# A feed-forward block in three-part products: another exact split, whose three products add up in one bank

## The chip, the cores and the metric

One core of one Trainium2 chip runs the whole kernel. The metric is the device time of one execution in microseconds (us). TensorE (PE) multiplies matrices, VectorE (DVE), ScalarE (ACT) and GpSimd (POOL) work element by element, and SyncE (SP) issues DMAs. PE writes its sums into PSUM, eight banks of 512 numbers per partition; DVE and ACT read them there.

## The reference

Random features of queries and keys make a linear attention, whose output x (4352 tokens by 128) goes through a gated feed-forward block with 1536 hidden channels:

```python
phi(x) = (S1 x) outer (S2 x)                    # 8 x 8 = 64 features per token and head
x = (phi(q) @ (phi(k).T @ v)) / (phi(q) @ sum(phi(k)) + 1e-6)
g = x @ w_gate
out = (g * (1.0 / (1.0 + np.exp(-g))) * (x @ w_val)) @ w_out
```

Everything is float32; the weights come as float64 and are narrowed on the chip.

## The kernel before

Tokens go in ten blocks: three of 384, 320 and 384 (blocks 0 to 2, batch 0), six of 480 (3 to 8) and one of 384 (9, `LAST`). The hidden channels go in twelve chunks of 128. A *unit* (i, j) is block i and chunk j: gate and value products into two neighbouring banks (a *pair*), Silu of the gate on ACT into `sg`, and the product of `sg` with the value on DVE into a slot of `hidden`. `down` takes the oldest unit from `todo` and adds its share of the output product into a bank of the block. Three pairs (banks 0 and 1, 4 and 5, 6 and 7) go round, the least recently used first (`pair`, L122); a unit holds its pair until `let_go` (L133). Banks 2 ("g2") and 3 ("acc") take the output sums. Attention for batches 1 to 3 runs between the units, step by step (`attentions`, L620): key features on DVE, their sums on POOL (L552), `fold` (L606 to L613), which makes the weights of the query sketches (L347), the sketches' copies on ACT (L595), `query_step` (L757 to L774) and `numerators` (L782), which takes two pairs, 64 small products (L792) and copies into `xT` (L809).

A float32 product of 480 columns is two passes of 0.405 us on PE (L1095). Blocks 0 and 1 and chunks 0 to 5 of block 2 are made so (`unit`, L1035). From unit (2, 6) on, gate and value products are made of *parts* that fit a shorter number format (F32R), in one pass of 0.217 us each. With B = 4096, each weight is w = w1 + wb/B and each token x = x1 + x0; wd = w1 - wb and xd = x1/B - x0. Then w x is (1 + 1/B) times the sum of w1 x1, wb x0 and -wd xd / (1 + 1/B). Of the output products, the 61 units listed in `DOWN` are made in the same way, with parts h1, h0, hd of the hidden unit.

- `start_unit` (L1001) makes both wd xd (L1007), and ACT scales the pair in place (L1010). `finish_unit` (L1012) adds w1 x1 (L1019) and wb x0 (L1020) for gate and value, then Silu (L1022) and product (L1027). In the main loop, unit y + 1 is started before unit y is finished, but at y = 20 and 40 (`WIDE`).
- `cut_weights` (L855) makes the parts of three chunks, one step at a time: w1 (ACT, L859), the rest (L862, DVE or POOL), wb (ACT, L864), wd (L867 on DVE, or L871 on POOL for v0, v2, v3 and g0). The steps are set out by hand in `steps_at` (L1347 to L1399).
- `cut_tokens` (L873) makes the parts of a block's tokens in two steps: x1 on ACT (L881) with x0 (L884, POOL or DVE) and xd (L889, DVE); `token_steps` (L1424) sets the steps of the later blocks, `cuts["x"]` and `x_steps` those of blocks 2 and 3.
- `cut_down` (L925) makes the parts of the output weights; its later steps are in `behind`.
- `cut_hidden` (L960) makes the parts of a unit's output a unit or two later: h1 (ACT L976, or DVE L980), h0 (DVE L984), and hd either on DVE (L990) or, where `carried`, by two DMAs: SP copies h1 to hd (L978) and POOL's accumulating DMA adds h0 (L988).
- `down` (L1072) puts wd hd (L1087) into the block's bank and w1 h1, wb h0 (L1089, L1090) into a second bank of the block, which lies in the other block's bank. ACT copies the second one out with a scale (`copy_out`, L1113), DVE joins both (`put_together`, L1123), and `store` transposes (DVE, L1147) and sends.

The main loop (L1429) runs 84 units, y = 0 to 83, for blocks 3 to 9. `before` and `behind` hold what is to be recorded ahead of or after a unit y. A unit's output product comes when more than 6 units wait (7 at the y in `LONGER`), so some 6 units later. All engines take their instructions in the order in which the code records them. PE's order is that of the code: `group()` at the y in `GROUPS`, the unit's products, then up to two output products.

```python
if y in WIDE:
    finish_unit(*at[0], y)
if y + 1 < END:
    start_unit(*at[1])
if y not in WIDE:
    finish_unit(*at[0], y)
```

Of the kernel before, what the change touches and what calls it, by code (L numbers as in the profile page):

```python
# [19 lines left out]
def kernel(  # L20
# [807 lines left out]
    CUT = 1.0 - 2.0**-13  # L828
    WHOLE = 1.0 + 1.0 / BETA
# [25 lines left out]
    def cut_weights(w, c, low, engine):  # L855

        w1, wb, wd = w_parts[id(w), c] = home(w, c)
        src = w[:, 3 * c : 3 * c + 3, :]
        nc.scalar.activation(out=w1, in_=src, func=AF.Copy, scale=CUT)  # L859
        yield  # L860
        low = low[0]
        engine.tensor_tensor(out=low, in0=src, in1=whole(w1), op=ALU.subtract)  # L862
        yield
        nc.scalar.activation(out=wb, in_=low, func=AF.Copy, scale=BETA)  # L864
        yield
        if engine is nc.vector:
            nc.vector.scalar_tensor_tensor(  # L867
                out=wd, in0=low, scalar=-BETA, in1=whole(w1), op0=ALU.mult, op1=ALU.add
            )
        else:  # L870
            engine.tensor_tensor(out=wd, in0=whole(w1), in1=whole(wb), op=ALU.subtract)  # L871

    def cut_tokens(i, engine=nc.gpsimd, soon=False):  # L873

        t0, n = blocks[i]
        x = xT[:, t0 : t0 + n]
        x1, x0, xd = x_parts[i] = [
            apool.tile([P, WB], F32R, tag=tag, name=name, bufs=2)
            for tag, name in (("qb", "x1"), ("dT", "x0"), ("rd", "xd"))
        ]  # L880
        nc.scalar.activation(x1[:, 0:n], x, AF.Copy, scale=CUT)  # L881

        def low():
            engine.tensor_tensor(  # L884
                out=x0[:, 0:n], in0=x, in1=whole(x1[:, 0:n]), op=ALU.subtract
            )

        def difference():
            nc.vector.scalar_tensor_tensor(  # L889
                out=xd[:, 0:n], in0=whole(x1[:, 0:n]), scalar=WHOLE, in1=x,  # L890
                op0=ALU.mult, op1=ALU.subtract,
            )


        first, second = (difference, low) if soon else (low, difference)
        first()
        yield
        second()
# [26 lines left out]
    def cut_down():  # L925
# [6 lines left out]
        def high(c):  # L932
            nc.scalar.activation(w1[:, c], wo[:, FINE[0] :][:, c], AF.Copy, scale=CUT)

        def left(c):
            nc.gpsimd.tensor_tensor(
                out=wb[:, c], in0=whole(w1[:, c]), in1=wo[:, FINE[0] :][:, c], op=ALU.subtract
            )

        def differ(c):  # L940
            nc.vector.scalar_tensor_tensor(
                out=wd[:, c], in0=whole(wb[:, c]), scalar=BETA, in1=whole(w1[:, c]),
                op0=ALU.mult, op1=ALU.add,
            )

# [6 lines left out]
        add_to(behind, 2, lambda: left(a))  # L952
        add_to(behind, 2, lambda: left(b))
        add_to(behind, 5, lambda: differ(a))
        add_to(behind, 6, lambda: differ(b))
        add_to(behind, 2, lambda: left(c))
        add_to(behind, 21, lambda: differ(c))
        yield

    def cut_hidden(y, i, j):  # L960
# [11 lines left out]
        small = -CUT / BETA  # L972
        carried = i in line[:3] and (i, j) not in [(line[2], 2), (line[2], 8)] or i in line[3:-1] and j % 2
        aside = carried or j % 2 or i in line[:3]
        if aside:
            add_to(behind, y + 1, lambda: nc.scalar.activation(h1, h, AF.Copy, scale=small))  # L976
        if carried:
            add_to(behind, y + 1, lambda: nc.sync.dma_start(out=whole(hd), in_=whole(h1)))  # L978
        if not aside:
            high = lambda: nc.vector.tensor_scalar(h1, h, small, None, op0=ALU.mult)  # L980
            before.setdefault(y + 1, []).insert(0, high)

        def rest():
            nc.vector.scalar_tensor_tensor(  # L984
                out=h0, in0=whole(h1), scalar=BETA, in1=h, op0=ALU.mult, op1=ALU.add
            )
            if carried:
                nc.gpsimd.dma_start(out=hd, in_=h0, accum_op=ALU.add)  # L988
            else:
                nc.vector.tensor_tensor(out=hd, in0=whole(h1), in1=whole(h0), op=ALU.add)  # L990
# [8 lines left out]
    sums_of = {}  # L999

    def start_unit(i, j):  # L1001

        n = blocks[i][1]
        xd = x_parts[i][2][:, 0:n]
        ps = sums_of[i, j] = pair((i, j))[:, :, 0:n]
        for k, w in enumerate((wg, wv)):
            nc.tensor.matmul(  # L1007
                ps[:, k], w_parts[id(w), j // 3][2][:, j % 3, :], xd, start=True, stop=True
            )
        nc.scalar.activation(ps, ps, AF.Copy, scale=-1.0 / WHOLE)  # L1010

    def finish_unit(i, j, y=None):  # L1012
        n = blocks[i][1]
        x1, x0, _ = (x[:, 0:n] for x in x_parts[i])
        ps = sums_of.pop((i, j))
        now(before, y)
        for k, w in enumerate((wg, wv)):
            w1, wb = (w_parts[id(w), j // 3][t][:, j % 3, :] for t in range(2))
            nc.tensor.matmul(ps[:, k], w1, x1, start=False, stop=False, skip_group_check=True)  # L1019
            nc.tensor.matmul(ps[:, k], wb, x0, start=False, stop=True, skip_group_check=True)  # L1020
        sg = fpool.tile([P, WB], FP32, tag="sg", name="sg", bufs=5)[:, 0:n]
        nc.scalar.activation(sg, ps[:, 0], AF.Silu, scale=WHOLE)  # L1022
# [4 lines left out]
        nc.vector.scalar_tensor_tensor(  # L1027
            out=hj[:, 0:n], in0=ps[:, 1], scalar=WHOLE, in1=sg, op0=ALU.mult, op1=ALU.mult
        )
        let_go((i, j))  # L1030
        now(behind, y)
        if (i, j) in DOWN:
            cut_hidden(y, i, j)
# [38 lines left out]
    def down(y=None):  # L1072
# [7 lines left out]
        mine = [c for c in range(NCH) if (i, c) in DOWN]  # L1080
        if mine and j == mine[0]:
            acc[i, "p"] = bank("acc" if i in line[0::2] else "g2")
        sides = dict(start=first, stop=(made[i] == NCH))
        if j in mine:
            w1, wb, wd = [down_parts[x][:, FINE.index(j), :] for x in ("w1", "wb", "wd")]
            h1, h0, hd = h_parts.pop((i, j))
            nc.tensor.matmul(acc[i][:, 0:n], wd, hd, **sides)  # L1087
            p = acc[i, "p"][:, 0:n]
            nc.tensor.matmul(p, w1, h1, start=(j == mine[0]), stop=False)  # L1089
            nc.tensor.matmul(p, wb, h0, start=False, stop=(j == mine[-1]))  # L1090
            h_free.extend(h_sets.pop((i, j)))
            if j == mine[-1]:
                copy_out(y, i, n)
        else:
            nc.tensor.matmul(acc[i][:, 0:n], wo[:, j, :], hidden[i, j][:, 0:n], **sides)  # L1095
# [3 lines left out]
        if made[i] == NCH:  # L1099
            if mine:  # L1100
                put_together(y, i, n)
            elif i == HEAD - 1:

# [3 lines left out]

    def copy_out(y, i, n):

        x = fpool.tile([P, WB], FP32, tag="sg", name="sum2", bufs=5)[:, 0:n]  # L1110
        p = acc[i, "p"][:, 0:n]
        acc[i, "p"] = x
        copy = lambda: nc.scalar.activation(x, p, AF.Copy, scale=-BETA * WHOLE)  # L1113
        if i == LAST or made[i] == NCH:
            copy()
        else:
            add_to(behind, y + 1, copy)

    def put_together(y, i, n):

        d, x = acc.pop(i)[:, 0:n], acc.pop((i, "p"))
        acc[i] = x
        join = lambda: nc.vector.tensor_tensor(out=x, in0=d, in1=x, op=ALU.add)  # L1123
        if i == LAST:
            join()
            store(i, n)
        else:
            add_to(before, y + 1, join)
            add_to(before, y + (2 if i != line[0] else 5), lambda: store(i, n))
# [201 lines left out]
    cuts = {"x": cut_tokens(2, nc.vector, soon=True)}  # L1331
# [16 lines left out]
    for z, (i, j) in enumerate(seq):  # L1348
# [21 lines left out]
        7: ("x",), 8: ("x", "g3", "v0"), 9: ("g0",),  # L1370
    }
    ND = 13
    for n in range(ND):
        if n == ND - 2:
            start_unit(2, 6)
# [11 lines left out]
    for j in range(6, NCH):  # L1387
        if j + 1 < NCH:
            start_unit(2, j + 1)
        finish_unit(2, j)  # L1390
# [9 lines left out]
    while todo:  # L1400
        if len(todo) == 2:
            start_unit(HEAD, 0)
# [3 lines left out]
        if len(todo) == 7:  # L1406
            parts_of(1)
            x_steps = cut_tokens(HEAD, nc.vector, soon=True)
# [12 lines left out]
    GROUPS, WIDE, EASY = (4, 6, 20, 22, 40), (20, 40), 20  # L1421
    LONGER = (18, 38, 72, 73, 74, 75)

    token_steps = {}  # L1424
    for m, i in enumerate(line[1:], 1):
        gen = cut_tokens(i)
        for at in {1: (3, 8), 2: (20, 21), 3: (27, 32), 4: (40, 42)}.get(m, (NCH * m - 10, NCH * m - 9)):
            token_steps.setdefault(at, []).append(gen)
    for y in range(END):  # L1429
# [5 lines left out]
        at = [(line[x // NCH], x % NCH) for x in (y, y + 1) if x < END]  # L1435
# [58 lines left out]
```

## Time and profile before

| | us |
|---|---|
| runs shown: lowest, median, highest | 273.53, 273.88, 274.0 |
| the profiled execution's own time | 273.72 |
| its span (first to last instruction) | 272.0 |
| PE busy | 265.8 |
| DVE busy | 223.3 |
| ACT busy | 199.6 |
| POOL busy | 87.5 |
| granted TensorE clock, whole span | 1.00 of full speed |

The page has a part for each engine's busy time, one for the chain of work that ended last, and groups of instructions by line. The timeline gives start and duration of each instruction; the end of a product on PE is modelled, so products follow each other from start to start, not from end to start. The table by stage has, for each stretch, the sum of busy time (and the count of instructions) of PE, weight loads (PEld), DVE, ACT and POOL, then the granted clock, the share of the DMA engines and GB/s. PE's first part product (L1007) stands at 72.39 us, unit (3, 0), y = 0, at 90 us, and y = 83 ends near 264 us.

### The profile page before, as it was taken

What the parts mean: (1) busy time and instruction counts of PE and PEld (TensorE: products, weight loads), DVE (VectorE), ACT (ScalarE), POOL (GpSimd) and SP (SyncE); (2) the same over time, 40 slices, a digit from 0 to 9 for tenths busy, and PEclk for the clock granted to TensorE, in tenths of its full rate; (3) what the DMA queues carried; (4) which work ended last, traced back from release to release, by engine and by line L of the source; (5) the groups of instructions that cost most, each with busy time, mean ns of one, the idle gap of its engine ahead of it and who ended that gap; (6) DMA issues with size and microseconds to landing.
All of it is one profiled execution on the core that took longest, in us unless ns stands there. A gap on an engine that the chain in (4) does not pass through costs nothing.

```text
span 272.0 us, 6028 instructions
## 1 busy us (share of the span) xinstructions
PE 265.8 (98%) x2212; PEld 204.0 (75%) x2212; DVE 223.3 (82%) x429; ACT 199.6 (73%) x357; POOL 87.5 (32%) x110
## 2 busy tenths in 40 slices
PE   8899999999999999999999999999999999999994
PEld 7645566666785687886677878867888888889994
DVE  3997988989788798987767889768968996998881
ACT  3468666362686789787579998869989888888870
POOL 3313422249431494470042342223224213222000
PEclk9999999999999999999999999999999999999999
DMA  6573197131331047811137869754476566647221
GB/s 194 172 212 95 49 260 215 40 127 29 94 90 27 1 120 189 180 49 39 39 88 178 177 140 187 180 108 123 86 160 155 118 136 147 146 103 153 39 36 29
DMA packets 36509, 32.01 MB, mean 118 GB/s; under 512 B 20992, under 2 KB 34560, under 8 KB 36480
## 3 DMA queue, kind: packets, MB, share of 16 engines
q1 hardware_dynamic: 30064, 22.13, 28.3%
q0 software_dynamic: 5184, 8.85, 19.0%
q10 hardware_dynamic: 1232, 0.66, 0.9%
q8 instruction: 17, 0.28, 0.4%
q14 instruction: 12, 0.10, 0.1%
HBM read 11.41 MB, written 2.23 MB: 50 GB/s over the span
## 4 chain that ended last, share of the span: by engine, by line
PE 92%; DVE 3%; DMA 2%; ACT 1%; issue 0%; SPq 0%; ACTq 0%
PE PS L1095 14%; PE PS L1019 14%; PE PS L1007 14%; PE PS L1020 14%; PE PS L1043 12%; PE PS L1087 5%; PE PS L1089 5%; PE PS L1090 5%; PE PS L359 2%; PE PS L792 2%; PE PS L347 2%; PE PS L393 2%; DMA kld<-in_k_dram 2%; PE PS L1133 1%; PE PS L502 1%; PE PS L450 1%
## 5 line engine op out<-in xcount | busy, mean ns | idle before, releaser
L1010 ACT ACTIVATE PS<-PS 128x960 f32<-128x960 f32 (+1 forms) x90 | 83.4, 926 | 22.1 <-PE PS L1007 20.6
L1027 DVE SCALAR_TENSOR_TENSOR hbuf<-PS,sg 128x480 f32<-128x480 f32 (+1 forms) x81 | 51.8, 639 | 21.2 <-ACT sg L1022 20.1
L1022 ACT ACTIVATE sg<-PS 128x480 f32<-128x480 f32 (+1 forms) x90 | 49.6, 552 | 2.2 <-PE PS L1020 1.9
L1007 PE MATMUL PS<-xd,wd 128*128 128x480 f32 (+1 forms) x90 | 33.6, 373 | 0.0
L1020 PE MATMUL PS<-x,wb 128*128 128x480 f32 (+1 forms) x90 | 33.5, 372 | 0.0
L1019 PE MATMUL PS<-x,w 128*128 128x480 f32 (+1 forms) x90 | 33.3, 370 | 0.0
L1095 PE MATMUL PS<-hbuf,wo 128*128 128x480 f32 (+3 forms) x80 | 33.0, 505 | 0.0
L1007 PE MATMUL PS<-xd,graw 128*128 128x480 f32 (+1 forms) x69 | 32.6, 472 | 0.0
L1020 PE MATMUL PS<-x,graw 128*128 128x480 f32 (+1 forms) x69 | 25.5, 370 | 0.0
L1043 PE MATMUL PS<-xT,wg 128*128 128x384 f32 (+1 forms) x60 | 23.5, 474 | 0.1
L1043 PE MATMUL PS<-xT,wv 128*128 128x384 f32 (+1 forms) x60 | 23.1, 467 | 0.3 <-DVE wv L288 0.3
L1007 PEld LDWEIGHTS PS<-xd,wd 128*128 128x128 f32 x90 | 16.9, 188 | 6.3 <-issue 2.3
L1047 ACT ACTIVATE sg<-PS 128x384 f32<-128x384 f32 (+1 forms) x24 | 11.2, 468 | 13.2 <-PE PS L1043 12.4
L1019 PEld LDWEIGHTS PS<-x,w 128*128 128x128 f32 x90 | 16.9, 187 | 2.2
L1020 PEld LDWEIGHTS PS<-x,wb 128*128 128x128 f32 x90 | 16.9, 188 | 2.1
L1019 PE MATMUL PS<-x,graw 128*128 128x480 f32 (+1 forms) x48 | 18.0, 376 | 0.0
L1095 PEld LDWEIGHTS PS<-hbuf,wo 128*128 128x128 f32 x80 | 14.8, 189 | 3.8 <-issue 0.4
L1007 PEld LDWEIGHTS PS<-xd,graw 128*128 128x128 f32 x69 | 13.0, 188 | 5.3 <-ACT PS L1010 1.9
L1043 PEld LDWEIGHTS PS<-xT,wv 128*128 128x128 f32 x60 | 11.2, 190 | 7.4 <-DVE hbuf L1058 0.8
L1043 PEld LDWEIGHTS PS<-xT,wg 128*128 128x128 f32 x60 | 10.9, 190 | 7.7 <-issue 1.1
L1019 PE MATMUL PS<-x,gphq 128*128 128x480 f32 (+1 forms) x42 | 16.1, 384 | 0.1
L1020 PEld LDWEIGHTS PS<-x,graw 128*128 128x128 f32 x69 | 13.0, 188 | 1.3
(287 smaller groups left out, 589.5 us busy)
## 6 DMA issues: line engine op xcount, KB each, us to landing
kld<-in_k_dram SPq DMA_DIRECT2D x4, 544.0 KB, 4.2
qld<-in_q_dram SPq DMA_DIRECT2D x3, 544.0 KB, 5.3
raw<-in_moe_w_out_dram SPq DMA_DIRECT2D x4, 384.0 KB, 4.6
hwv<-hwv POOLq DMA_DIRECT2D x6, 240.0 KB, 3.5
hextra<-hextra POOLq DMA_DIRECT2D x6, 240.0 KB, 3.5
vld<-in_v_dram SPq DMA_DIRECT2D x9, 144.0 KB, 5.2
hwv<-hwg SPq DMA_DIRECT2D x5, 240.0 KB, 3.0
hkld<-hqld SPq DMA_DIRECT2D x5, 240.0 KB, 2.5
```

The source lines that it names most:

```text
L1007: nc.tensor.matmul(ps[:, k], w_parts[id(w), j // 3][2][:, j % 3, :], xd, start=True, stop=True)
L1010: nc.scalar.activation(ps, ps, AF.Copy, scale=-1.0 / WHOLE)
L1019: nc.tensor.matmul(ps[:, k], w1, x1, start=False, stop=False, skip_group_check=True)
L1020: nc.tensor.matmul(ps[:, k], wb, x0, start=False, stop=True, skip_group_check=True)
L1022: nc.scalar.activation(sg, ps[:, 0], AF.Silu, scale=WHOLE)
L1027: nc.vector.scalar_tensor_tensor(out=hj[:, 0:n], in0=ps[:, 1], scalar=WHOLE, in1=sg, op0=ALU.mult, op1=ALU.mult)
L1043: nc.tensor.matmul(o[:, 0:n], w[:, j, :], xT[:, t0 : t0 + n], start=True, stop=True)
L1047: nc.scalar.activation(sg[:, 0:n], g[:, 0:n], AF.Silu)
L1087: nc.tensor.matmul(acc[i][:, 0:n], wd, hd, **sides)
L1089: nc.tensor.matmul(p, w1, h1, start=(j == mine[0]), stop=False)
L1090: nc.tensor.matmul(p, wb, h0, start=False, stop=(j == mine[-1]))
L1095: nc.tensor.matmul(acc[i][:, 0:n], wo[:, j, :], hidden[i, j][:, 0:n], **sides)
```

## The change

The parts are cut otherwise. With P = 1 - 1/B: w1 is w times (1 + 2^-13) in the short format, wd = -B (w - w1), wb = w1/B + (w - w1); x1 likewise, xd = x - x1 and x0 = (x - P x1) (B + 1/P). Then w x is P times the plain sum of w1 x1, wd xd and wb x0. So all three go into one bank, with no scaling by ACT between, and P is put into Silu's scale and the product's. `start_unit` and `finish_unit` become one `fine_unit`, which makes six products in the order w1 x1, wd xd, wb x0 for gate, then for value (interleaved where `mixed`). No unit is begun one ahead. `down` adds its three into the block's one bank; `copy_out` and `put_together` go, and `store` reads that bank.

The last step of `cut_weights` is on DVE for all chunks. `cut_tokens` has a third step on ACT (the lift of x0). `cut_down` has six more operations on ACT, and its last ones come at y = 8 and 9, not 21. `cut_hidden` cuts h1 on ACT always; SP copies h itself to hd as soon as it is made, POOL's accumulating DMA adds h1, and two more units are `carried`. The y 72 to 75 leave `LONGER`.

```diff
 def cut_weights(w, c, low, engine):
-    nc.scalar.activation(out=wb, in_=low, func=AF.Copy, scale=BETA)
-    yield
-    if engine is nc.vector:
-        nc.vector.scalar_tensor_tensor(
-            out=wd, in0=low, scalar=-BETA, in1=whole(w1), op0=ALU.mult, op1=ALU.add
-        )
-    else:
-        engine.tensor_tensor(out=wd, in0=whole(w1), in1=whole(wb), op=ALU.subtract)
+    nc.scalar.activation(out=wd, in_=low, func=AF.Copy, scale=-BETA)
+    yield
+    nc.vector.scalar_tensor_tensor(
+        out=wb, in0=whole(w1), scalar=1.0 / BETA, in1=low, op0=ALU.mult, op1=ALU.add
+    )
 def cut_tokens(i, engine=nc.gpsimd):
     def low():
+        nc.vector.scalar_tensor_tensor(
+            out=x0[:, 0:n], in0=whole(x1[:, 0:n]), scalar=-PART, in1=x,
+            op0=ALU.mult, op1=ALU.add,
+        )
+    def difference():
         engine.tensor_tensor(
+            out=xd[:, 0:n], in0=x, in1=whole(x1[:, 0:n]), op=ALU.subtract
+        )
+    difference()
+    yield
+    low()
+    yield
+    nc.scalar.activation(x0[:, 0:n], whole(x0[:, 0:n]), AF.Copy, scale=LIFT)
...
 def cut_down():
         def differ(c):
+            nc.scalar.activation(wd[:, c], whole(wb[:, c]), AF.Copy, scale=-BETA)
             nc.vector.scalar_tensor_tensor(
+                out=wb[:, c], in0=whole(w1[:, c]), scalar=-1.0 / BETA, in1=whole(wb[:, c]),
                 op0=ALU.mult, op1=ALU.add,
             )
+        def lift(c):
+            nc.scalar.activation(wb[:, c], whole(wb[:, c]), AF.Copy, scale=LIFT)
+        for x, y in ((a, 5), (b, 6), (c, 8)):
+            add_to(behind, y, lambda x=x: differ(x))
+            add_to(behind, y + 1, lambda x=x: lift(x))
 def cut_hidden(y, i, j):
-        carried = i in line[:3] and (i, j) not in [(line[2], 2), (line[2], 8)] or i in line[3:-1] and j % 2
+        carried = i in line[:3] or i in line[3:-1] and j % 2
         if carried:
-            add_to(behind, y + 1, lambda: nc.sync.dma_start(out=whole(hd), in_=whole(h1)))
+            add_to(behind, y, lambda: nc.sync.dma_start(out=whole(hd), in_=h))
+        def high():
+            nc.scalar.activation(h1, h, AF.Copy, scale=-CUT)
+            if carried:
+                nc.gpsimd.dma_start(out=hd, in_=whole(h1), accum_op=ALU.add)
+        add_to(behind, y + 1, high)
         def rest():
             nc.vector.scalar_tensor_tensor(
+                out=h0, in0=whole(h1), scalar=PART, in1=h, op0=ALU.mult, op1=ALU.add
+            )
+            if not carried:
+                nc.vector.tensor_tensor(out=hd, in0=h, in1=whole(h1), op=ALU.add)
+def fine_unit(i, j, y=None, mixed=False):
+    now(before, y)
+    marks = [(k, t) for k in range(2) for t in (0, 2, 1)]
+    if mixed:
+        marks.sort(key=lambda x: (0, 2, 1)[x[1]])
+    for k, t in marks:
+        nc.tensor.matmul(
+            ps[:, k], w_parts[id((wg, wv)[k]), j // 3][t][:, j % 3, :], xs[t],
+            start=(t == 0), stop=(t == 1),
+        )
+    nc.scalar.activation(sg, ps[:, 0], AF.Silu, scale=PART)
...
 def down(y=None):
+        if (i, j) in DOWN:
+            ws = [down_parts[x][:, FINE.index(j), :] for x in ("w1", "wb", "wd")]
+            for t, w, h in zip(range(3), ws, h_parts.pop((i, j))):
+                nc.tensor.matmul(
+                    acc[i][:, 0:n], w, h, start=(first and t == 0), stop=(last and t == 2)
+                )
...
-    LONGER = (18, 38, 72, 73, 74, 75)
+    LONGER = (18, 38)
-    for at in {1: (3, 8), 2: (20, 21), 3: (27, 32), 4: (40, 42)}.get(m, (NCH * m - 10, NCH * m - 9)):
+    for at in {1: (3, 8, 9), 2: (20, 21, 22), 3: (27, 32, 33), 4: (40, 42, 43)}.get(m, range(NCH * m - 10, NCH * m - 7)):
-        if y in WIDE:
-            finish_unit(*at[0], y)
-        if y + 1 < END:
-            start_unit(*at[1])
-        if y not in WIDE:
-            finish_unit(*at[0], y)
+        fine_unit(line[y // NCH], y % NCH, y, mixed=(y == 0))
```

Scales and signs left out here change with the split. `fine_unit` writes the product for `LAST` in two pieces where a unit is in `DOWN`.

More of the change, by code (lines that the diff above doesn't have):

```diff
@@ L827 @@
     BETA = 4096.0
-    CUT = 1.0 - 2.0**-13
-    WHOLE = 1.0 + 1.0 / BETA
+    CUT = 1.0 + 2.0**-13
+    PART = 1.0 - 1.0 / BETA
+    LIFT = BETA + 1.0 / PART
     w_parts = {}
@@ L951, in cut_down @@
         high(c)
[L952 to L957, printed above, removed]
+        for x in (a, b, c):
+            add_to(behind, 2, lambda x=x: left(x))
+        for x, y in ((a, 5), (b, 6), (c, 8)):
+            add_to(behind, y, lambda x=x: differ(x))
+            add_to(behind, y + 1, lambda x=x: lift(x))
         yield
@@ L1003, in start_unit @@
         n = blocks[i][1]
-        xd = x_parts[i][2][:, 0:n]
-        ps = sums_of[i, j] = pair((i, j))[:, :, 0:n]
-        for k, w in enumerate((wg, wv)):
+        xs = [x[:, 0:n] for x in x_parts[i]]
+        ps = pair((i, j))[:, :, 0:n]
+        now(before, y)
[3 more added lines that the diff above has]
+        for k, t in marks:
             nc.tensor.matmul(
-                ps[:, k], w_parts[id(w), j // 3][2][:, j % 3, :], xd, start=True, stop=True
-            )
@@ L1010, in start_unit @@
[L1010 to L1020, printed above, removed]
+                ps[:, k], w_parts[id((wg, wv)[k]), j // 3][t][:, j % 3, :], xs[t],
@@ L1026, in finish_unit @@
         todo.append((i, j))
-        nc.vector.scalar_tensor_tensor(
-            out=hj[:, 0:n], in0=ps[:, 1], scalar=WHOLE, in1=sg, op0=ALU.mult, op1=ALU.mult
-        )
+        cut = (i, j) in DOWN
+        m = (SPLIT if i == LAST else n) if cut else 0
+        for a, b, scale in ((0, m, PART * PART), (m, n, PART)):
+            if a < b:
+                nc.vector.scalar_tensor_tensor(
+                    out=hj[:, a:b], in0=ps[:, 1, a:b], scalar=scale, in1=sg[:, a:b],
+                    op0=ALU.mult, op1=ALU.mult,
+                )
         let_go((i, j))
+        if cut:
+            cut_hidden(y, i, j)
         now(behind, y)
-        if (i, j) in DOWN:
-            cut_hidden(y, i, j)
     def unit(i, j, late=False, between=(None, None), apart=False):
@@ L1079, in down @@
         made[i] = made.get(i, 0) + 1
[L1080 to L1090, printed above, removed]
+        last = made[i] == NCH
+        if (i, j) in DOWN:
[4 more added lines that the diff above has]
+                )
             h_free.extend(h_sets.pop((i, j)))
-            if j == mine[-1]:
-                copy_out(y, i, n)
-        else:
-            nc.tensor.matmul(acc[i][:, 0:n], wo[:, j, :], hidden[i, j][:, 0:n], **sides)
+        else:
+            nc.tensor.matmul(
+                acc[i][:, 0:n], wo[:, j, :], hidden[i, j][:, 0:n], start=first, stop=last
+            )
         if i != LAST:
@@ L1098, in down @@
             slots.append(slot_of[i, j])
-        if made[i] == NCH:
-            if mine:
-                put_together(y, i, n)
+        if last:
+            if HEAD <= i < LAST:
+                add_to(before, y + 1, lambda: store(i, n))
             elif i == HEAD - 1:
@@ L1106, in down @@
                 store(i, n)
[L1108 to L1129, printed above, removed]
     def straight(ps, j):
@@ L1330 @@
     lows = {}
-    cuts = {"x": cut_tokens(2, nc.vector, soon=True)}
+    cuts = {"x": cut_tokens(2, nc.vector)}
     for c in (2, 3, 0, 1):
@@ L1407 @@
             parts_of(1)
-            x_steps = cut_tokens(HEAD, nc.vector, soon=True)
+            x_steps = cut_tokens(HEAD, nc.vector)
             next(x_steps)
```

44 lines of the change are left out of this document (7 added, 37 removed).

## The prediction

> **What bounds the kernel now.** I read the page first, then the table by stage, then TensorE's timeline, then the chain, then VectorE's timeline.
>
> ```profile
> PE 265.8 (98%) x2212; PEld 204.0 (75%) x2212; DVE 223.3 (82%) x429; ACT 199.6 (73%) x357; POOL 87.5 (32%) x110
> ...
> PE 92%; DVE 3%; DMA 2%; ACT 1%; issue 0%; SPq 0%; ACTq 0%
> ...
> L1010 ACT ACTIVATE PS<-PS 128x960 f32<-128x960 f32 (+1 forms) x90 | 83.4, 926 | 22.1 <-PE PS L1007 20.6
> ```
>
> TensorE (PE) is busy for 98% of the span and makes 92% of the chain that ended last. ScalarE (ACT) spends 83.4 of its 199.6 us on the scaling at L1010 that the change takes out, but it is on that chain for 1% only.
>
> ```profile
> 190.00:244.00 54.00, 54.00 (x247) 46.01 (x246) 48.37 (x85) 47.93 (x73) 14.54 (x16) 1.00 0.60 130
> ```
>
> From 190 to 244 us PE is busy all of the time at granted clock 1.00, though VectorE (DVE, 48.37) and ScalarE (47.93) are nearly full. A busy record could hide waits, so I read the distance from start to start in PE's timeline:
>
> ```profile
> 157.67 0.37 PE L1019 MATMUL PS<-x,w 128*128 128x480 f32 x1
> 157.88 0.38 PE L1020 MATMUL PS<-x,wb 128*128 128x480 f32 x1
> 158.24 0.49 PE L1087 MATMUL PS<-hqld,dparts 128*128 128x480 f32 x1
> 158.56 0.38 PE L1089 MATMUL PS<-hkT,dparts 128*128 128x480 f32 x1
> 158.78 0.38 PE L1090 MATMUL PS<-hkT,dparts 128*128 128x480 f32 x1
> ```
>
> Undisturbed parts products of 480 columns start 0.217 us apart (median 217 to 219 ns in each of L1007, L1019, L1020, L1087, L1089, L1090; 175 ns for 384 columns). Here the steps 0.36 and 0.32 show a stall, 0.25 us with its refill. Adding step minus median over each 10 us, PE loses under 0.05 us in each stretch of 110 to 130, 160 to 170 and 190 to 240. **So only single stalls can be won.** They are, after 80 us:
>
> - 82.0: 0.14, behind L1010
> - 93 to 97: 0.20 in three, behind L1010, in units of 1.3 us, where ScalarE needs 0.958 + 0.568 = 1.53
> - 138.8 to 139.3: 0.24, behind L1010
> - 158.2: 0.25, behind a landing (below)
> - 179 to 181: 0.60, numerators
> - 183.9: 0.37, behind L1010 (0.49 - 0.217, and 0.10 in the next step)
>
> ```profile
> 133.73 1.48 PE PS L792 x38
> ...
> 179.16 2.08 PE PS L792 x39
> 181.27 0.71 ACT xT L809 x2
> 182.93 0.97 ACT PS L1010
> 183.94 0.48 PE PS L1019
> ```
>
> The chain, in order of time, gives the numerators at 1.48 undisturbed and 2.08 at 179. There one pair of banks is held for a unit already begun, so the two pairs that L792 needs are the ones just written; PE waits for ScalarE and VectorE to empty them. The sum of the list is **1.80 us**.
>
> **What is removed.** PE's list has 1657 products in both kernels, of the same shapes: nothing is won in its work. It now adds three products in a row in one bank; that is no unknown, since L1019 to L1020 (same bank) step as L1020 to L1019 (next bank), 218 and 217 ns. ScalarE loses 90 x 926 ns and 7 copies at 0.57; it gains 19 cuts of the hidden part at 0.60, 8 lifts of tokens at 0.60 and 6 operations on down parts at some 0.55: net about -68 us. VectorE loses 19 cuts at 0.41, 7 joins at 0.65 and 2 additions at 0.66; it gains 4 weight parts at 0.55 and 8 short pieces. All of it runs beside PE, so I take it at 0 apart from the listed stalls. Those behind L1010 lose their cause; at 179 and 183.9 no pair is held any more, and the next unit takes the pair of the unit before the numerators, emptied 1.5 us later. What is late next is the emptying of a pair: it ends 1.1 to 2.4 us after the unit's last product, and a pair is used again three units on, 3.9 us at the shortest. I take all 1.55 us of these; bounds 1.0 and 1.55.
>
> **What is moved: the carried differences.** Today ScalarE writes h1 a unit later, SP copies it, VectorE makes h0, and GpSimd (POOL) issues the accumulating DMA. Now SP copies h as soon as VectorE has it, and POOL issues after ScalarE's cut. For unit (7, 1), h was ready at 202.16, SP issued at 203.96, landed at 207.22, POOL issued at 207.78, landed at 211.40, wanted at 212.59. The copy starts 1.8 us sooner, and POOL needs ScalarE's cut only, which ends at about 204. So landings come about 1.8 us sooner. The thinnest margins now, 0.04 (the stall at 158.2), 0.34 and 0.48 us, all grow: 0.25 us won, bounds 0 and 0.25. SP's later loads and stores queue behind a copy that waits for VectorE at most one unit, and POOL's token subtraction behind an accumulation that waits for a copy (2.2 to 4.3 us to land). The subtraction has two to four units of 2 us until use; if that cover went, a unit would start up to 2 us late. Two more DMA pairs are carried. Without the entries 72 to 75 of LONGER, the products of (8, 6) to (8, 9) come one unit (1.7 us) sooner, which the 1.8 us balance. The third token step is two units or more ahead of its use and hidden there; at the head, (3, 0) multiplies x0 last, some 2 us after its lift. The tail is the same: the last product, the copy, the last stores.
>
> **What is added on the path: VectorE from 67 to 86 us.** The last weight part of v2, v3, v0 and g0 moves from POOL to VectorE.
>
> ```profile
> 67.81 0.57 DVE L1147 STREAM_TRANSPOSE o<-PS 128x384 f32<-128x384 f32 x1
> 68.31 0.59 DVE L867 SCALAR_TENSOR_TENSOR graw<-room,graw 128x384 fp32r<-128x384 f32 x1
> 69.09 0.23 DVE L606 TENSOR_TENSOR fold<-PS,sq 128x64 f32<-128x64 f32 x1 [0.19 <-PE PS L718]
> 69.35 0.27 DVE L610 TENSOR_REDUCE w<-fold 128x8 f32<-128x64 f32 x1
> 69.65 0.23 DVE L613 TENSOR_TENSOR s<-w,own 128x64 f32<-128x64 f32 x1
> ...
> 84.18 0.97 DVE L774 STREAM_TRANSPOSE phT<-phq 128x768 f32<-128x768 f32 x1
> ```
>
> Two of them (v2, v3) stand ahead of L606. Today L613 ends at 69.88 and PE's sketches (L347) start at 70.83: 0.95 us of slack, and 0.19 idle ahead of L606. Each part costs 0.47 of the queue (0.55 with its overlap) to 0.99 (the same line at 65.88, with POOL busy). 2 x 0.47 is under 0.95 + 0.19; 2 x 0.99 is 0.84 over. I take one of each, 1.46: **0.3 us** of stall, bounds 0 and 0.85. One row speaks for the dear price of the first: POOL's last sum runs from 67.55 to 68.49, and the L889 that met POOL took 1.19 against 0.55 for the next one. The Trainium skill, SBUF — State Buffer, "Who interferes with whom", says that a VectorE instruction with two SBUF inputs and a GpSimd instruction that reads SBUF exclude each other for a whole instruction. By that rule the first part starts 0.64 us late, at 68.49, and the second meets an idle POOL, so the stall would be about 0.4 (0.64 + 2 x 0.47 - 1.14); the trace agrees, in that L889 ended 0.42 us after POOL's operation did at 70.73.
>
> Behind it, ScalarE's lift of x0 for block 2 waits for VectorE; behind the lift are a first cut (0.42) and the two copies of the query sketches (0.57 each), so the denominators start 1.0 to 1.5 us late (73.03 now). VectorE then alternates a unit's product (0.47) with 0.87 to 0.95 of attention, in units of 1.59, with 0.9 idle until 84. Adding v0 and g0 (0.94) and that lateness, and taking off this idle and the 0.4 that a unit is emptied sooner without L1010 (products of (2, 10) end at 81.45, its Silu starts at 81.85), the last L774 ends 0.6 to 1.1 after 85.15. L792 starts at 85.53 now, 0.38 after it, and would be 0.3 later anyway by the first stall: from the middle, 0.85 - 0.68, **0.15 us** of stall; bounds 0 and 2.06 (if none is absorbed: 0.94 + 1.5 - 0.38).
>
> **The sum.** -1.55 - 0.25 + 0.3 + 0.15 = -1.35 us. The profiled execution took 273.72 us with a span of 272.0, and the rest stays: 272.4. The median of the runs is 273.88, 0.16 above it; between both footings I say **272.5**.
>
> **The rivals.** (1) The gain is given back in the queue of VectorE: the stalls at 70.8 and 85.5 together reach 1.3 to 2.3 us, and the time is 273.3 to 274.4. For it: VectorE has no idle from 59 to 69. Against: the removed scaling lets each unit be emptied sooner. 0.18. (2) Slower: the same queue at its dearest. If weight parts take 0.99 each and the late lift delays the query copies by all of it, PE stalls 0.85 + 2.06; against 1.8 won this gives 274.8. It decides from 2.35 us of new stalls on. Against: POOL, whose operations make the 0.99, has nothing to run after 68.49 once its own two parts (2.29 us from 68.44) are gone. 0.14. (3) The scaling's stalls hid other ones, and only the 0.85 us of the numerators and the landing goes, less 0.45 added: 273.3. 0.08. (4) All of it goes and nothing new appears: 271.9, 0.10. My forecast, 272.0 to 273.2, has 0.50. That the change doesn't do what it says is excluded by the lists: L1010 is absent, products are alike.
>
> **Chances.** 0.2% is 0.55 us, about what a measurement can tell here. Faster (forecast, (4), half of (3), and the part of (1) at its edge): 0.67; within 0.2%: 0.18; slower: 0.15. The range, 271.7 to 274.4, takes in (4) and (1) and leaves out (2).
>
> **What would show it.** Right: numerators at 179 in about 1.48; no step over 0.3 us after 90; L978's copies issued within 0.3 us of h; ScalarE near 132 us busy. Wrong: PE waiting for VectorE at L347 or L792 by over 1.3 us together; steps of 0.217 us becoming longer where three products share a bank; POOL waiting for copies so long that a unit waits for xd.

## The result and the profile after

| | before | after |
|---|---|---|
| median of the runs, us | 273.94 (273.53 to 274.0) | 272.11 (271.95 to 272.45) |
| ratio after to before, 95% interval | | 0.9938 [0.9921, 0.9955] |
| the profiled execution, its span, us | 273.72, 272.0 | 272.45, 270.7 |

The changed kernel is faster by 1.83 us of the medians, 0.6%; the interval allows 1.2 to 2.2. Three single executions of the kernels below were far longer (343.85, 532.53 and 296.51 us) and are left out of the ratios. The page of after, with the lines that answer to those of before (L1012 is now the Silu; the scaling has no line any more):

```profile
PE 263.4 (97%) x2212; PEld 204.4 (75%) x2212; DVE 215.6 (80%) x413; ACT 138.4 (51%) x293; POOL 84.5 (31%) x108
...
PE 87%; DVE 8%; DMA 2%; ACT 1%; issue 1%; SPq 0%; DVEq 0%; ACTq 0%
...
L1012 ACT ACTIVATE sg<-PS 128x480 f32<-128x480 f32 (+1 forms) x90 | 50.0, 555 | 78.4 <-PE PS L1007 73.9
```

ScalarE lost 61 us of work, and the time fell by less than two: it was beside PE before and is now. It sits idle 73.9 us ahead of Silu, waiting for the products. VectorE has 8% of the chain now, up from 3%; from 64.7 to 69.4 us the chain runs through its weight parts, towards the one new wait. The row of the table by stage from 190 to 244 us (PE, weight loads, VectorE, ScalarE and GpSimd busy, then clock, DMA share, GB/s):

```profile
190.00:244.00 54.00, 54.00 (x247) 46.00 (x246) 42.69 (x69) 29.74 (x57) 14.33 (x16) 1.00 0.61 135
```

PE has the same 247 products in the same 54.00 us; ScalarE went from 47.93 to 29.74, VectorE from 48.37 to 42.69. Nothing is won here, since nothing was waited for here. What was won is single waits. From the chain of after, in order of time, the first of three stretches of sketches (L347) and all three of numerators (L792):

```profile
71.55 1.69 PE PS L347 x72
...
86.22 1.48 PE PS L792 x38
...
133.62 1.48 PE PS L792 x38
...
178.64 1.48 PE PS L792 x38
```

The numerators at 179 take 1.48 us, before 2.08. The one new wait stands ahead of the first sketches: the timeline shows 0.21 us of idle time there, and by the steps it costs 0.28 (PE goes from its last product into the sketches in 0.64 us, before in 0.36).

**One measure for what follows.** The start up to about 66 us varies between executions by 0.5 us (the first keys took 4.25 us to land in the profile of before and 4.74 in that of after). So beside the time I use a *stretch* of PE's timeline: from the first product of L393 of batch 1, at 66.36 us before, to the end of the last product. It is 202.03 us before and 200.40 after: 1.63 less. The span fell by 1.3 only, as the start of after's profiled execution was 0.5 later; its 272.45 is the highest of its four runs. Each kernel has one trace that counts here, but where kernels do the same work the parts of the stretch agree closely: from the first numerators to the next keys (L792 to L393) it is 11.39 us in the changed kernel and in three of its variants below. The ratios are coarser: their intervals are 0.3 to 0.7% wide, 0.9 to 1.8 us, so a gain below 1 us is read from the stretch and the rows, not from a ratio.

### The profile page after: what moved, and what is told of

Its sections match the earlier page's. It is cut to its first block, busy times and chain, and to the rows that moved or that the text cites. A ratio compares the mean times of both kernels' runs of the same rounds, so it can differ in the third digit from the quotient of the medians.

```text
span 270.7 us, 5871 instructions
## 1 busy us (share of the span) xinstructions
PE 263.4 (97%) x2212; PEld 204.4 (75%) x2212; DVE 215.6 (80%) x413; ACT 138.4 (51%) x293; POOL 84.5 (31%) x108
## 4 chain that ended last, share of the span: by engine, by line
PE 87%; DVE 8%; DMA 2%; ACT 1%; issue 1%; SPq 0%; DVEq 0%; ACTq 0%
PE PS L1007 42%; PE PS L1079 14%; PE PS L1084 11%; PE PS L1038 10%; PE PS L347 2%; DMA kld<-in_k_dram 2%; PE PS L792 2%; PE PS L359 1%; PE PS L393 1%; DVE phk L382 1%; PE PS L1100 1%; DVE room L863 1%; PE PS L502 1%; PE PS L450 1%; DVE exp L273 1%
## 5 line engine op out<-in xcount | busy, mean ns | idle before, releaser
L1012 ACT ACTIVATE sg<-PS 128x480 f32<-128x480 f32 (+1 forms) x90 | 50.0, 555 | 78.4 <-PE PS L1007 73.9
L1021 DVE SCALAR_TENSOR_TENSOR hbuf<-PS,sg 128x480 f32<-128x480 f32 (+2 forms) x83 | 52.0, 628 | 26.6 <-ACT sg L1012 19.9
L1007 PE MATMUL PS<-x,graw 128*128 128x480 f32 (+1 forms) x117 | 49.0, 418 | 0.0
L1007 PE MATMUL PS<-x,gphq 128*128 128x480 f32 (+1 forms) x63 | 26.3, 417 | 0.0
L1007 PEld LDWEIGHTS PS<-x,graw 128*128 128x128 f32 x117 | 22.0, 188 | 5.3 <-ACT sg L1012 1.5
L1007 PE MATMUL PS<-xd,graw 128*128 128x480 f32 (+1 forms) x69 | 25.5, 370 | 0.0
L1007 PEld LDWEIGHTS PS<-x,gphq 128*128 128x128 f32 x63 | 11.8, 188 | 3.5 <-issue 1.3
L1079 PE MATMUL PS<-hextra,dparts 128*128 128x480 f32 (+1 forms) x31 | 9.7, 371 | 0.0
```

Of the source, the lines that this page charges most:

```text
L1007: nc.tensor.matmul(ps[:, k], w_parts[id((wg, wv)[k]), j // 3][t][:, j % 3, :], xs[t], start=(t == 0), stop=(t == 1),)
L1012: nc.scalar.activation(sg, ps[:, 0], AF.Silu, scale=PART)
L1021: nc.vector.scalar_tensor_tensor(out=hj[:, a:b], in0=ps[:, 1, a:b], scalar=scale, in1=sg[:, a:b], op0=ALU.mult, op1=ALU.mult,)
L1079: nc.tensor.matmul(acc[i][:, 0:n], w, h, start=(first and t == 0), stop=(last and t == 2))
```

## The experiments

They ask three things: which part of the change took the waits away, whether the new ones are where the prediction put them, and what comes next when PE's list itself is cut. All ratios are to the kernel before, on the same chip as the experiment.

### The scaling alone, taken out of the kernel before

```diff
-        nc.scalar.activation(ps, ps, AF.Copy, scale=-1.0 / WHOLE)
```

> The kernel before, with the scaling at L1010 left out and nothing else changed (so the computation lacks the factor -1/WHOLE on wd xd). Theory: the scaling is the cause of the waits listed in the prediction at 82, 93 to 97, 138.8, 179 to 181 and 183.9 us (1.55 us in sum); they go, the landing at 158.2 (0.25) stays, and the stall of 0.22 at L347 does not come, as POOL keeps its weight parts: 273.9 - 1.55 = 272.4, ratio 0.994. Rival (the held pair, not the scaling, lengthens the numerators): they stay at 2.08, 0.95 are won, 272.95, ratio 0.9965. Second rival (the scaling's waits covered other waits of the same size): within 0.3 us of the kernel before.

Measured: ratio 0.9943 [0.9923, 0.9963]; the stretch is 200.95, 1.08 less than before. All waits behind L1010 are gone (by stretches of PE's timeline 0.40 us up to 95, 0.24 at 139 and 1.05 from 179 on, 1.69 in all), and the numerators take 1.48 with the pair still held. So the first theory holds and the rival of the held pair falls. But 0.60 us came back, so the stretch won 1.08 us and not the 1.55 of the theory; that the ratio is 0.994 all the same is within its interval, and no proof of the sum. From the chain of this kernel:

```profile
158.39 3.79 DMA hkld<-hkld
162.23 0.48 PE PS L1086
...
179.08 1.48 PE PS L792 x38
```

At 162.23 PE waits 0.40 us, 0.50 with its refill, for an accumulating DMA that was issued at 158.39, and at 157.68 it loses 0.17 to the one ahead: 0.41 more from 141 to 179 than before, where one landing cost 0.25. So units that come sooner meet landings that do not. With the scaling gone the landings cost about 0.66 us, not the 0.25 that the kernel before showed; in the changed kernel, with its earlier copies, no product waits for a landing after 80 us.

The other 0.19 is lost from 103 to 133, by a wait of the same kind, for VectorE. Its sum of hidden parts (L984) stands beside a GpSimd operation (L884, 101.20 to 102.44 here) and takes 1.53 us, without the scaling and in the kernel before alike:

```profile
101.43 1.53 DVE L984 SCALAR_TENSOR_TENSOR hwg<-hwg,hbuf 128x480 fp32r<-128x480 f32 x1
```

```profile
101.61 1.53 DVE L984 SCALAR_TENSOR_TENSOR hwg<-hwg,hbuf 128x480 fp32r<-128x480 f32 x1
```

Measured from the start of the stretch, the unit product behind it comes 0.13 us sooner than before and PE 0.40, and PE waits 0.24 for that product in the middle of the sketches, at 103.58. The scaling had hidden this wait.

### The unit begun one ahead, put back into the changed kernel

```diff
-        fine_unit(line[y // NCH], y % NCH, y, mixed=(y == 0))
...
+        if y in (20, 40):
+            fine_unit(*at[0], y)
+        if y + 1 < END:
+            begin(*at[1])
+        if y not in (20, 40):
+            fine_unit(*at[0], y, mixed=(y == 0))
```

`begin` puts the two products w1 x1 of unit y + 1 ahead of the other products of unit y, so one pair is held at the numerators as before.

> The changed kernel, but in the main loop units are begun one ahead again: the two products w1 x1 of unit y + 1 stand ahead of the rest of unit y (not at y = 20 and 40), so that a unit holds its pair of banks twice as long. There is no scaling. If the held pair was the cause of the longer numerators at 179 us, L792 at y = 40 takes about 2.1 us again instead of 1.48, and the time rises by 0.6 us, to 272.7; nothing else moves. If the wait came from ScalarE's load, the numerators stay at 1.48 and the time at 272.1.

Measured: ratio 0.9916 [0.9882, 0.9949], where the changed kernel has 0.9938. Nothing is lost. The same kernel once more, for its trace:

> The changed kernel, with the units begun one ahead again (the first two products of each unit are put ahead of the rest of the unit before, and the numerators find one pair of banks held), for its trace. If the held pair made the numerators at 179 us long (my theory in the prediction): L792 at y = 40 takes 2.0 to 2.1 us, with PE waiting for ScalarE or VectorE. If it was the scaling at L1010 alone, which delayed the Silu of y = 39 by 0.97 us (rival): 1.48 us here too, since that scaling is gone.

```profile
178.34 1.48 PE PS L792 x38
```

The stretch is 200.22 us, as in the changed kernel within 0.2. So without the scaling a held pair costs nothing, and dropping the begun unit won nothing by itself. The cause of the 0.60 at 179 is read in the kernel before, in ScalarE's timeline:

```profile
177.52 0.97 ACT L1010 ACTIVATE PS<-PS 128x960 f32<-128x960 f32 x1
178.41 0.57 ACT L1022 ACTIVATE sg<-PS 128x480 f32<-128x480 f32 x1
```

The Silu of unit y = 39 (its products end near 177.9) stands behind the scaling of unit y = 40, and VectorE's product follows it from 179.01 to 179.67. L792 needs that unit's pair. VectorE's own parts of the hidden unit before (L980, L984) stand ahead of that product too, and had been made late by the scaling one unit earlier: VectorE is idle for only 0.17 us ahead of it. With the scaling left out and the pair still held, the product starts at 178.32. In after the same Silu runs from 176.77 to 177.34 and the product ends at 178.09, ahead of the numerators at 178.57.

### Not begun ahead, in the kernel before

```diff
-        if len(todo) == 2:
-            start_unit(HEAD, 0)
...
-        if y in WIDE:
-            finish_unit(*at[0], y)
-        if y + 1 < END:
-            start_unit(*at[1])
-        if y not in WIDE:
-            finish_unit(*at[0], y)
+        start_unit(*at[0])
+        finish_unit(*at[0], y)
```

> The kernel before, with its units not begun one ahead: the product of wd and xd of a unit stands directly ahead of the unit's own scaled products. Theory: TensorE then waits in each unit for the scaling at L1010, which takes 0.958 us for 960 columns and starts after the product, less what the second product of the pair and its fill cover: 0.7 to 1.0 us for each of some 84 units, 60 to 85 us in all, 335 to 360 us. So what was begun ahead served the scaling alone, and the changed kernel may drop it since its bank needs no operation between the products. Rival: ScalarE is so free then that other work covers it, under 20 us.

Measured, in one execution: 384.82 us, 110.5 more than the one of the kernel before beside it (274.28); both numbers of the expectation were too low. From the timeline, one unit of it:

```profile
266.02 0.38 PE L1007 MATMUL PS<-xd,wd 128*128 128x480 f32 x1
...
266.44 0.95 ACT L1010 ACTIVATE PS<-PS 128x960 f32<-128x960 f32 x1 [0.40 <-PE PS L1007]
...
267.44 0.48 PE L1019 MATMUL PS<-x,gphq 128*128 128x480 f32 x1 [1.04 <-ACT PS L1010]
...
267.76 0.38 PE L1020 MATMUL PS<-x,gphq 128*128 128x480 f32 x1
```

From the second product's start to the next product's it is 1.42 us where 0.217 is the step, and the step after is 0.32: 1.31 us for this unit. Over all units it is 1.33 on average for the 72 of 480 columns and 1.18 for the twelve of 384, 110 us in sum (some of it is the clock: granted 0.79 from 100 to 120 us here, 1.00 after that). I had priced the wait by the scaling's duration less cover; but ScalarE starts only when the product has ended (0.42 after its start), and PE refills after it. So the begun unit served the scaling, and with the scaling gone it serves nothing. The numerators of y = 40 take 1.51 us here, with every scaling in place but no unit begun: the long ones before needed both, a unit begun ahead and its scaling ahead of another unit's Silu.

### ScalarE's load, without the place between products

The changed kernel with a copy of 2n columns ahead of each Silu (a store that nobody reads):

```diff
+        nc.scalar.activation(
+            sg.bitcast(mybir.dt.bfloat16), wo[:].rearrange("p c d -> p (c d)")[:, 0 : 2 * n], AF.Copy
+        )
```

> The changed kernel with ScalarE's old load, but not its place in the chain: ahead of each Silu of the 90 part units, ScalarE copies two blocks' width of the output weights (960 or 768 columns) to a place that nobody reads. If waits behind the scaling were the loss, PE sees nothing of it as long as pairs are emptied within three units: 272.1 to 272.5, with ScalarE busy for some 210 us. If ScalarE's load as such cost the time, the 1.0 to 1.5 us come back: 273.1 to 273.6.

Measured: ratio 0.9962 [0.9942, 0.9983], between the two expectations; the stretch is 201.53, 1.13 more than the changed kernel. ScalarE is busy for 215.5 us, more than the 199.6 of the kernel before, as the cuts of h1 are on it too. 0.22 of the 1.13 is at the numerators of 85 us, where VectorE's L774 came late; 0.89 is at one place, PE at 253.80:

```profile
244.28 1.00 ACT L1012 ACTIVATE sg<-wo 128x960 bf16<-128x960 f32 x1
245.31 0.57 ACT L1015 ACTIVATE sg<-PS 128x480 f32<-128x480 f32 x1
```

```profile
253.80 0.48 PE L1082 MATMUL PS<-hkT,dparts 128*128 128x480 f32 x1 [0.63 <-DMA hkT<-hextra]
```

With the copy, a unit costs ScalarE 1.99 us with its cut of h1 (starts at 240.31, 242.30, 244.28), and PE 1.95. It falls behind, until the Silu of unit (8, 11) ends at 245.88, 3.8 us after its last product started (242.12). SP's copy goes out at 246.60, GpSimd's accumulation at 250.63, and PE waits. Between 90 and 250 us nothing is lost, though ScalarE is busy for 52.82 of the 54 us from 190 to 244. So none of the waits behind L1010 came back with the load: what made PE wait there was the scaling's place, between two products of a bank and ahead of another unit's Silu. But the load is not free: put on the changed kernel, it takes 1.13 of the 1.63 us back, at two other places.

### The two weight parts ahead of the fold, moved behind it

```diff
-        0: ("g2", "v2", "v3"), 1: ("g2",), 2: ("g2", "g3"), 3: ("g3", "v2"), 4: ("g3", "v3"), 5: ("g2",),
-        7: ("x",), 8: ("x", "g3", "v0"), 9: ("x", "g0"),
+        0: ("g2", "v2", "v3"), 1: ("g2",), 2: ("g2", "g3"), 3: ("g3",), 4: ("g3",), 5: ("g2",),
+        7: ("x",), 8: ("x", "g3", "v0", "v2"), 9: ("x", "g0", "v3"),
```

> The changed kernel, with the last weight part of v2 and v3 put behind the fold in VectorE's order (one and two steps later) instead of ahead of it. If these two parts cause the wait ahead of the query sketches (L347), which the trace of the changed kernel shows as some 0.22 us, the sketches start without a wait and the time falls by 0.2 us, to 271.9. If the fold waits for something else there, nothing changes. If the parts are now late for unit (2, 6) or (2, 9), a wait shows there and the time rises.

Measured: ratio 0.9916 [0.9883, 0.9949], which cannot show 0.2 us (the kernel with units begun ahead has the same ratio); stretch 200.12, 0.28 less than the changed kernel, all of it at L347. The wait is gone. First the changed kernel, VectorE's timeline and the sketches that wait for it:

```profile
68.31 1.08 DVE L867 SCALAR_TENSOR_TENSOR wb<-w,room 128x384 fp32r<-128x384 f32 x1
...
70.25 0.54 DVE L867 SCALAR_TENSOR_TENSOR wb<-w,room 128x384 fp32r<-128x384 f32 x1
70.72 0.21 DVE L606 TENSOR_TENSOR fold<-PS,sq 128x64 f32<-128x64 f32 x1
```

```profile
71.55 1.20 PE L347 MATMUL PS<-s,qT 128*32 128x96 f32 x48 [0.21 <-DVE s L613]
```

And with the two parts behind the fold:

```profile
69.12 0.23 DVE L606 TENSOR_TENSOR fold<-PS,sq 128x64 f32<-128x64 f32 x1 [0.20 <-PE PS L718]
```

```profile
70.80 1.45 PE L347 MATMUL PS<-s,qT 128*32 128x96 f32 x60
```

In the changed kernel the fold starts with no idle time ahead of it and L347 shows 0.21 idle; here the fold has 0.20 to spare again and L347 none.

### Less work for PE: five and nine more units by parts

```diff
+    DOWN += [(line[0], j) for j in (9, 10)] + [(line[1], 5), (line[2], 3), (line[2], 7)]
```

Each such unit costs PE three products of 0.217 instead of two of 0.405, and VectorE, ScalarE, SP and GpSimd one operation each more.

> The changed kernel, with the output products of five more units, (3, 9), (3, 10), (4, 5), (5, 3) and (5, 7), made of parts: each takes 3 x 0.217 us on PE instead of 0.81. If PE's own work is the bound and the other engines have room after the change, the time falls by 5 x 0.16 = 0.8 us, to 271.3. If VectorE is the bound between 92 and 130 us (35.5 us busy of 38), the numerators of y = 20 wait and 0.3 or less of it is left.

Measured: ratio 0.9917 [0.9885, 0.9949], by itself not to be told from the changed kernel's 0.9938; stretch 199.56, 0.85 less than the changed kernel: PE's saving, 5 x (0.81 - 0.65), and nothing more waits. With the two weight parts behind the fold as well:

> The changed kernel with both earlier edits: the last weight part of v2 and v3 behind the fold, and five more units whose differences are carried by parts. Theory (PE's list is the bound, and the two edits touch different places): both gains add up, 0.3 + 0.8 = 1.1 us below the changed kernel, about 271.0. Rival (they draw on the same idle time of VectorE): one of the two only, 271.3 to 271.8, with a wait for VectorE at the numerators of y = 20.

Measured: ratio 0.9904 [0.9887, 0.9921], about 271.3 on the footing of 273.94. Once more, for its trace:

> The changed kernel with the last weight part of v2 and v3 behind the fold and five more units by parts, for its trace. Theory: no wait at L347 at 70 us (its step as usual, 0.09), no wait at the numerators of y = 20 or y = 40 (1.48 us), VectorE's L382 and L774 at 0.94 to 0.97 us there, and the way from the first keys of batch 1 to the end of the last product 1.1 us shorter than in the changed kernel (200.40), 199.3. Rival: GpSimd's sums are pushed behind waiting accumulations as in the kernel with nine units, and VectorE's operations beside them take 1.4 to 2.1 us.

It took 271.04; its stretch is 199.26, and L347 at 70 us and L792 at 132 and 177 are undisturbed. Both gains add up (1.14 less than the changed kernel). This is the fastest version of the study. But VectorE is now full ahead of y = 20. The rows of the table by stage from 110 to 130 us, of the changed kernel and of this one:

```profile
110.00:130.00 20.00, 20.00 (x85) 15.70 (x84) 18.16 (x28) 7.39 (x13) 7.88 (x7) 1.00 0.32 70
```

```profile
110.00:130.00 20.00, 20.00 (x89) 16.31 (x88) 19.90 (x30) 8.61 (x16) 8.83 (x9) 1.00 0.49 110
```

VectorE went from 18.16 to 19.90 of 20 us, and its last L774 ends 0.63 us ahead of these numerators, in the changed kernel 1.19. With nine units in place of five, (3, 11) and (4, 1) to (4, 3) being the new ones:

> As the kernel with both edits, but nine units carried by parts in place of five. Theory (0.16 us of PE for each unit, VectorE still with room): another 0.64 us, 270.4. Rival (VectorE has no room left in 92 to 132 us, where it has 0.7 to 1.8 us idle in each 18 to 20): the last L774 ahead of the numerators at y = 20 comes late, PE waits 0.3 to 1 us there, and the time is that of five units or up to 0.4 more.

Measured: ratio 1.006 [1.0042, 1.0079], slower than the kernel before; the stretch is 202.78, 3.52 more than with five. From its timelines of PE, GpSimd and VectorE:

```profile
136.24 1.18 PE L792 MATMUL PS<-phT,spread 32*32 32x288 f32 x39 [2.58 <-DVE phT L774]
```

```profile
119.18 1.60 POOL L552 TENSOR_TENSOR zs<-late 128x512 f32<-128x512 f32 x1
121.88 0.87 POOL L981 DMA_DIRECT2D hsoon<-hwv  x1 [1.11 <-DVE qab L764]
122.49 3.59 POOL L552 TENSOR_TENSOR zs<-zs,late 128x512 f32<-128x512 f32 x2
```

```profile
119.39 1.44 DVE L762 TENSOR_SCALAR den<-den 128x36 f32<-128x36 f32 x1
...
122.79 2.13 DVE L382 TENSOR_TENSOR phq<-qab 128x768 f32<-128x768 f32 x1
...
133.14 0.94 DVE L382 TENSOR_TENSOR phq<-qab 128x768 f32<-128x768 f32 x1
```

PE waits 2.58 us at the numerators, and 0.62 at 131 for a unit's pair. The four more sums of VectorE are 2.6 us, and with five units it had 0.1 idle from 110 to 130 and 0.63 of slack. The overlap comes on top: GpSimd's list is in order, and its sums (L552) now stand behind accumulations that wait for copies, and end at 130.1, where in the changed kernel they end at 121.6. As long as they run, VectorE's L382 takes 2.13 us, twice, and the small L762 1.44; with GpSimd idle, at 133.14, L382 takes 0.94, and in the changed kernel L762 takes 0.23: 2 x 1.19 and 1.21 are 3.6 us. With five units the same sums end at 125.4, L382 takes 1.48 once and L762 1.43, as the rival had it, and the slack ahead of y = 20 covers it. No run here moved GpSimd's sums alone, so the shares of the two causes stay open.

## Why the prediction was right, point by point

Predicted was 272.5 with a range of 271.7 to 274.4; measured 272.11. The interval of the gain, 1.2 to 2.2 us, cannot tell the forecast 1.35 from the 1.83 of the medians; the stretch can, and it gives 1.63. The mechanism was the forecast one: PE's waits behind L1010 and one landing go, and one wait ahead of L347 comes. Some terms were off, and one cause was wrong:

- *Waits behind L1010, at most 1.55 us.* All went: PE's loss falls from 1.49 to 1.16 us in 80 to 90, from 1.26 to 1.03 in 90 to 100, from 2.06 to 1.85 in 130 to 140 and from 2.08 to 1.13 in 170 to 190. The kernel without the scaling puts them at 1.69, a little over the bound. No product steps longer where three share a bank: 218 ns at 480 columns in after, 217 to 219 before. Right.
- *The numerators at 179 are long because one pair is held.* Wrong as a cause: with the pair held and no scaling they take 1.48 (two kernels show it). The wait was the Silu of y = 39 behind L1010. The prediction's own row at 133.73 spoke against the theory. Unit y = 20 had been begun at 130.64, so a pair was held there too, and the numerators took 1.48, as the product of the unit before had ended at 133.53. That the 0.60 came out in the sum is luck as far as the held pair goes: the change takes out the scaling with it.
- *Landings about 1.8 us sooner.* For unit (7, 1) the margin went from 1.19 to 3.03, 1.84 more. From the timelines of SP and GpSimd in after:

```profile
200.21 0.47 SPq L975 DMA_DIRECT2D hvld<-hbuf  x1
```

```profile
203.94 0.86 POOL L980 DMA_DIRECT2D hvld<-hextra  x1 [3.61 <-ACT hqT L978]
```

  SP's copy goes 0.03 us after h is made (200.18), before 1.80 after it. That the margin grew by just that is partly chance: h itself comes 1.98 us sooner, the use only 0.96, and the accumulating DMA landed 4.66 us after its issue, before 3.62. The thin margins grew more than I said, as h comes sooner without L1010 and hd is multiplied last of the three, 0.43 later: (4, 11) from 0.04 to 3.74, (6, 9) from 0.34 to 3.57, (8, 11) from 0.48 to 3.18. The thinnest is now 1.31, at (3, 2). And the term was mis-sized: 0.25 is what the landing cost while the scaling slowed the units; without the scaling it would have been about 0.66.
- *0.3 us at L347.* Measured 0.28, by the step into the sketches (0.64 us, before 0.36) and by what the two parts behind the fold gave back. The first part took 1.08 us beside GpSimd's last sum (68.05 to 68.98), the second 0.54 with GpSimd idle: one dear and one cheap, as taken. By the rule of the Trainium skill, SBUF — State Buffer, "Who interferes with whom", a VectorE operation with two SBUF inputs contends with a GpSimd operation that reads SBUF, and the one waits for the other; the trace agrees, as the first part's end at 69.39 is 0.41 after GpSimd's, not far from the 0.54 that the second takes alone.
- *0.15 us at L792 of 86.* Measured none: the last L774 ended at 85.99 and PE came at 86.22, later by the first wait. The bound of 2.06 was far from what happened.
- *ScalarE near 132 us busy.* Measured 138.4. By group, the removed operations are 87.2 us and the added ones 18.4, 68.8 net, near the forecast 68; the engine's busy time fell by 61.2 only, since records of neighbouring operations overlap and count once there. All records of ScalarE add up to 222.4 us before, where 199.6 are busy. A sum over groups is not a difference of engine times.
- *The sum.* The measured terms are 1.69 won behind L1010, 0.25 won at the landing and 0.28 lost at L347: 1.66, where the stretch fell by 1.63. The forecast 1.35 is short by the 0.15 that did not come and by 0.14 of the scaling's waits. PE's list has 2212 products in both profiles, of the same shapes, not 1657; nothing hangs on that number.
- *The signs.* 36 of the 38 copies go within 0.3 us of h, and the numerators take 1.48. But "no step over 0.3 us after 90" was a bad sign: behind a float32 product both kernels show a step of some 0.02 us and then one of 0.59 (120.39, 120.41 and 121.00 in after), together what two products take, and no wait.

The rivals: the first two (VectorE's queue) needed 1.3 to 2.9 us of new waits, and 0.28 came. The third (hidden waits) did not show in the changed kernel; in the kernel before without its scaling, though, 0.60 of 1.69 came back, so it was nearer than its 0.08 says. The fourth, 271.9, is 0.2 from the measured time, nearer than the forecast by less than the runs can tell; but its mechanism, that nothing new appears, is not what happened.

## What to carry to other kernels

When one engine is busy for 98% of the span, price an edit by the single waits it removes, read from the distance between starts, and not by the work it takes from other engines: here 61 us of ScalarE's were worth 1.6 us. An operation between two products of one bank costs twice, in the hand-over and as a plug ahead of other units' work; ask of each wait what stood ahead of the late instruction in its queue before blaming the buffer. When units come sooner, DMA landings do not, so the margin of each landing must be looked at again, and a DMA that waits in GpSimd's list moves the work behind it into VectorE's time. Before an edit is enlarged, look at the busy share of the engine it loads in the very stretch ahead of the next hand-over.

## What the runs showed that was not expected

- Beside a GpSimd operation even a small VectorE operation can take nearly as long as that one does: L762 on 128 x 36 numbers takes 0.17 to 0.18 us alone and 1.43 to 1.44 beside a sum on GpSimd, where it ended 0.05 after that sum in both kernels; L382 on 128 x 768 takes 0.94 alone and 1.48 to 2.13.
- In a kernel with a hand-over in each unit, PE loses more than the other engine's operation lasts: 1.31 us for a scaling of 0.95, by the product that must end first and the refill (0.1).
- Four more units by parts, after five that gained 0.85 us, lost 3.5 us by the stretch and 4.3 by the ratios. VectorE's share of the whole span does not show that the limit is near (82% in both); its share of the stretch ahead of the numerators does (19.90 of 20 us with five units).
